# A recurrent attention layer with streamed weights: left K cast by ScalarE, left queries copied amid the Exp, results stored straight from SBUF, streamed units at new places

## The chip, the cores and the metric

The kernel runs on one core of a Trainium2 chip. Its time is the device time of one execution in microseconds (us), the median of several runs. The core has five instruction queues: TensorE (PE, with its weight loads as PEld), VectorE (DVE), ScalarE (ACT), GpSimd (POOL) and SyncE (SP), and sixteen DMA engines that all of them share. SBUF is the memory next to the engines, PSUM the one into which TensorE writes[...].

## The reference, cut to what matters

Two layers run on the same normed input and are added to it. The first is a recurrence over 64 segments of 32 rows; each segment puts 8 memory rows in front, and the first 8 rows of its result are the memory of the next. It has 32 heads of 128. The second is a dense layer with GELU.

```python
for s in range(n_seg):                        # 64 segments of 32 rows
    xs = x[:, s * seg_len:(s + 1) * seg_len, :].copy()
    h = jnp.concatenate([mem, xs], axis=1)    # 8 + 32 rows
    q = jnp.einsum('btd,dhe->bhte', h, Wq)
    k = jnp.einsum('btd,dhe->bhte', h, Wk)
    v = jnp.einsum('btd,dhe->bhte', h, Wv)
    scores = jnp.einsum('bhqe,bhke->bhqk', q, k) * scale
    scores = jnp.where(mask[None, None], scores, -1000000000.0)
    p = _softmax(scores, axis=-1)
    o = jnp.einsum('bhqk,bhke->bhqe', p, v)
    o = jnp.einsum('bhte,hed->btd', o, Wo)
    mem = o[:, :M, :].copy()                  # memory of the next segment
    outs.append(o[:, M:, :])
...
xn = _layernorm(x, axis=-1)
return x + _A_ref(xn, ...) + _B_ref(xn, ...)
```

## The kernel before

The four weight matrices of the recurrence (8 MB each in bf16) don't fit in SBUF. They are cut into 64 units of 128 x 2048 bf16, 512 KB each: eight units for each half of K, Q and V and sixteen for O. In each segment TensorE goes through all 64. 46 units stay in SBUF; 18 are streamed through six slots, in the order in which they are used. Two of the 18 are kept in PSUM banks and copied back by VectorE (`start_stream`, `kept_in`) rather than read from HBM, and one (`PART`) has 768 of its 2048 columns kept in SBUF, so that 320 KB of it are read. A slot takes its next unit once TensorE is done with the last (`unit_done`).

A segment's 32 rows are computed as 24 rows and 8 "left" rows. The 24 and the 8 memory rows go through in every segment. The left rows of four segments (a group; `i4` counts 0 to 3 in it) go together, one weight half at a time, each in one of the four segments: Q0 in i4 = 1, Q1 in i4 = 2, K0 and V1 in i4 = 3, K1 and V0 in i4 = 0, O in i4 = 1. So the four kinds of segment have different work. "Left K" is the K of those rows, "left queries" their Q.

```python
LEAD = 6
LATER = 3
STREAM_BUFS = 6
AT_BANKS, AT_PART = 5, 4
PART_COLS = 768
...
PLACED = "SS.....S" "....S..." ".S...S.." ".S.....S" "....S..." ".S.S..S." "...S.S.S" "..S..SS."
IS_STREAMED = {unit: PLACED[n] == "S" for n, unit in enumerate(ORDER)}
...
IN_PSUM = [unit for unit in ORDER if IS_STREAMED[unit]][3]
STREAMED_O = [unit for unit in ORDER[48:] if IS_STREAMED[unit]]

IN_BANKS, PART = STREAMED_O[AT_BANKS], STREAMED_O[AT_PART]
KEPT = (IN_PSUM, IN_BANKS)
...
            unit = UNIT_AT[place]
            res_tiles[unit] = slab(place)[:, :]
            fetch(res_tiles[unit], unit)


    streams = [unit for _ in range(NSEG) for unit in ORDER if IS_STREAMED[unit]]
...
    used = 0

    def copy_bits(out, in_):

        nc.vector.tensor_single_scalar(out=out, in_=in_, scalar=0, op=ALU.bitwise_or)

    def start_stream(slot):
        if not starts:
            return
        n = starts.popleft()
        unit, t = streams[n], slab(slot)
        if unit in kept_in:
            for c0, bank in kept_in[unit]:
                copy_bits(t[:, c0:c0 + 1024].bitcast(U32), bank.bitcast(U32))
        elif unit == PART:
            nc.sync.dma_start(out=t[:, PART_COLS:], in_=copies[unit])
        elif unit in copies:
            nc.sync.dma_start(out=t[:, :], in_=copies[unit])
        else:
            fetch(t[:, :], unit)
        stream_tiles[n], slot_of[n] = t, slot
```

The three accumulator banks go round: a pass takes one (two with left rows), and whoever reads it out lets it go. `turn` reads a bank out and transposes the result; `q_left` copies eight left queries per head beside the segment's own, `keep_q` copies the rest of them into spare columns of the PSUM bank `mixed`.

```python
            def turn(ps, home, cp):

                rows_out(ps, home, cp)
                nc.vector.transpose(out=home, in_=home)

            ...
            def turn_kL(ps, u):
                kL[u] = sp.tile([P, 16, 32], BF16, name=f"kL{u}")
                turn(ps, kL[u][:, :, :], nc.vector.tensor_copy)

            ...
            def q_left(u):

                if i4 >= 2 + u and more:
                    q = qS[:, i4 - 2 - u, :, :]
                else:
                    q = qL[u][:, :, NL * i4:NL * i4 + NL]
                nc.vector.tensor_copy(out=q_home[:, :, 0:NL], in_=q)

            ...
            def keep_q(u):

                n = 2 - u
                copy_bits(
                    mixed[:, 340:340 + 64 * n].bitcast(U32).rearrange("p (i h t) -> p h i t", i=n, h=16),
                    qL[u].bitcast(U32)[:, :, (GRP - n) * NL // 2:].rearrange("p h (i t) -> p h i t", i=n),
                )
```

Scores, the Exp and the masks (the Exp writes `pr_all`, a part of the buffer `half_home`); then the sums, whose result is written to `pd_main`. Scores and sums both use the PSUM bank `mixed`.

```python
            def scores(u):

                ... # 32 matmuls into mixed[:, 0:224], of kT, kL[u] and q_home
                pr = pr_all[:, 0:224]
                nc.scalar.activation(out=pr, in_=mixed[:, 0:224], func=ACT.Exp, scale=INV_SQRT_DH)
                prA = pr[:, 0:160].rearrange("p (c q) -> p c q", q=40)
                prB = pr[:, 160:224].rearrange("p (c q) -> p c q", q=16)
                for p, m in ((prA[:, :, NL:SEG], mask_order), (prB, mask_left[:, i4, :])):
                    n = m.shape[-1]
                    nc.vector.tensor_tensor(out=p, in0=p, in1=m[:, None, :].to_broadcast([P, 4, n]), op=ALU.min)
                st["pr", u] = prA, prB

...
            def sums(u):
                prA, prB = st["pr", u]
                ... # 8 matmuls into mixed[:, 0:160], of prA and prB
                nc.scalar.activation(out=mixed[:, 0:160], in_=mixed[:, 0:160], func=ACT.Ln)

                for b in (1, 0):
                    nc.scalar.activation(
                        out=mixed[:, 160 * b:160 * b + 160], in_=mixed[:, 0:160], func=ACT.Exp, scale=-1.0,
                        bias=off[:, b:b + 1],
                    )
                pdA = pd_main.rearrange("p (c b q) -> p c b q", c=4, b=2)
                ...
                nc.vector.tensor_tensor(
                    out=pdA.rearrange("p c b q -> p b c q"), in0=prA[:, None, :, :].to_broadcast([P, 2, 4, 40]),
                    in1=dd, op=ALU.mult,
                )
```

The order of a segment's passes. `at` names what is done after which unit of a pass.

```python
            turn_k(psK, 0)
            if first:
                turn_kL(psKL, 0)
            at = {} if first else {1: [lambda: q_left(0)]}
            if left_q[0] and not first:
                at[2] = [lambda: keep_q(0)]
            psQ, psQL = half_pass("Q", 0, left_q[0], at)
            if first:
                turn_qL(psQL, 0)
                q_left(0)
            turn_q(psQ)
            if left_q[0] and not first:
                turn_qL(psQL, 0)
            psK1, psK1L = half_pass("K", 1, left_k[1], {})
            st["kT", 1] = nat_home
            rows_out(psK1, nat_home, nc.scalar.copy)
            at = {
                0: [lambda: scores(0), lambda: nc.vector.transpose(out=nat_home, in_=nat_home)],
                6: [lambda: sums(0)],
            }
            if not first:
                at[1] = [lambda: q_left(1)]
                if left_q[1]:
                    at[2] = [lambda: keep_q(1)]
            if left_k[1]:
                at.setdefault(1, []).append(lambda: turn_kL(psK1L, 1))
            psQ1, psQ1L = half_pass("Q", 1, left_q[1], at)
            if first:
                turn_qL(psQ1L, 1)
                q_left(1)
            turn_q(psQ1)
            if left_k[0] and not first:
                turn_kL(psKL, 0)
            if left_q[1] and not first:
                turn_qL(psQ1L, 1)
            psV, psVL = half_pass("V", 0, left_v[0], {})
            st["V", 0] = values_out(psV, sp.tile([P, 512], BF16, name="v", tag="a"), nc.scalar.copy)
            if left_v[0]:
                left_values(0, psVL)
...
```

The end of a segment: the O pass, the memory rows of the next segment, and the results. In i4 = 1 the result of the left rows (`resL`, in `pr_all`) and that of the main rows go to a staging tensor in HBM and from there to the output; in i4 = 2 the main rows are staged too.

```python
            if i4 == 3:
                at.setdefault(2, []).append(rows_of_main)
...
                if n == 1 and left_o:
                    st["resL"] = pr_all
                    nc.gpsimd.dma_start(out=st["resL"][:, :], in_=hrL_d[og, :, 256:512])
            nw = 2 if left_o else 1
...
            res, rows = st["res"], slice(s * SEG, s * SEG + NX)
            tiles = (res, st["resL"]) if left_o else (res,)
            for w, r in reversed(list(enumerate(tiles))):
                nc.vector.tensor_tensor(out=r[:, :], in0=psX[:, 256 * w:256 * w + 256], in1=r[:, :], op=ALU.add)
                if left_o and not final:

                    for b in range(2):
                        c0 = 256 * (2 * b + w)
                        nc.gpsimd.dma_start(out=outL_d[og, :, c0:c0 + 256], in_=r[64 * b:64 * b + 64, :])
            let_go(psX)
...
            elif left_o:
                pairs = [(out_flat[rows, :], outL_d[og, m0:m0 + NX, :])]
                pairs += [
                    (out_flat[row:row + NL, :], outL_d[og, NL * sl:NL * sl + NL, :]) for sl, row in left_rows
                ]
                for o, r in pairs:
                    small.append(lambda o=o, r=r: nc.gpsimd.dma_start(out=o, in_=r))
            elif i4 == 2:
                nc.gpsimd.dma_start(out=outM_d[g, :, :], in_=res[:, :])
                o = out_flat[rows, :].rearrange("t (j c) -> j t c", j=4)
                r = outM_d[g, :, :].rearrange("(j t) c -> j t c", j=4)[:, 0:NX, :]
                rows_of_main = lambda o=o, r=r: nc.sync.dma_start(out=o, in_=r)
            else:
                for j in range(4):
                    nc.gpsimd.dma_start(out=out_flat[rows, 256 * j:256 * j + 256], in_=res[32 * j:32 * j + NX, :])
```

## Time and profile before

Three runs took 1886.43, 1886.92 and 1889.38 us. The profiled execution has a span of 1889.4 us.

| engine | busy us | share of the span | instructions |
|---|---|---|---|
| PE (matmul) | 1720.6 | 91% | 32208 |
| PEld (weight load) | 935.8 | 50% | 32228 |
| DVE | 917.8 | 49% | 2222 |
| ACT | 634.8 | 34% | 1352 |
| POOL | 234.2 | 12% | 464 |

The DMA engines moved 614.17 MB, 325 GB/s over the span. How to read the lines below: in the slices, each digit is the busy share of a fortieth of the span in tenths. A group of instructions is given by line of the kernel, engine, operation, and out<-in by the program's names. A wait is given as who waited for whom, and then the total in us, how often, and the longest. "L706" is the matmul of the projections (in `product`), L901 that of the O pass, L808 and L814 the scores, L833 and L839 the sums, L750 the cast in `rows_out`, L764 the transpose in `turn`, L786 the copy in `q_left`, L820 the Exp of the scores, L854 the write of `pd_main`, L241 VectorE's copy `copy_bits` (into `u`: a kept unit into its slot; into `mixed`: `keep_q`), L1005 the cast of the memory rows at a segment's end, which serves as the mark between segments.

### The profile page before, as it was taken

To read this page: it belongs to the slowest core of one execution; us is meant where nothing else is said; L and a number is where in the kernel's file an instruction comes from. 1 tells how busy PE (TensorE), PEld (TensorE's weight loads), DVE (VectorE), ACT (ScalarE), POOL (GpSimd) and SP (SyncE) were. 2 spreads that over 40 slices of the span, in tenths; PEclk is the share of its full clock that TensorE was granted. 3 is DMA by queue.
4 is the path that set the end of the run, shared out by engine and by line. 5 is a ranking of instruction groups with operands and counts; after the bars stand their busy time and mean duration, and the time that the engine had idled before them with its cause. 6 is when DMAs were issued, how large, how long until landed. Compare 5 with 4: busy or idle time off the path is not lost. (4 is left out here: it accounts for less than half of the span.)

```text
span 1889.4 us, 72759 instructions
## 1 busy us (share of the span) xinstructions
PE 1720.6 (91%) x32208; PEld 935.8 (50%) x32228; DVE 917.8 (49%) x2222; ACT 634.8 (34%) x1352; POOL 234.2 (12%) x464
## 2 busy tenths in 40 slices
PE   7999999998899898888989999999898888999987
PEld 3444444444454555545555555555555454545544
DVE  6657474614354444444444444444445454444443
ACT  6334352502233333333333333333233333333333
POOL 0000000001341111111111110111111111111111
PEclk9999999999999999999999999999999999999999
DMA  9821211599999999999999999999999999999998
GB/s 340 264 52 44 55 47 50 172 360 357 340 389 395 362 381 373 377 368 369 381 378 386 381 388 385 398 386 382 362 380 374 373 365 380 370 383 383 374 374 322
DMA packets 219672, 614.17 MB, mean 325 GB/s; under 512 B 45547, under 2 KB 65435, under 8 KB 219356
## 3 DMA queue, kind: packets, MB, share of 16 engines
q1 hardware_dynamic: 200892, 590.16, 82.9%
q0 software_dynamic: 14368, 16.71, 2.7%
q8 instruction: 252, 4.13, 0.9%
q10 hardware_dynamic: 4096, 2.64, 0.5%
q14 instruction: 64, 0.52, 0.1%
HBM read 595.19 MB, written 30.28 MB: 331 GB/s over the span
## 5 line engine op out<-in xcount | busy, mean ns | idle before, releaser
L706 PE MATMUL acc<-u,hr_home 128*32 128x512 bf16 x11520 | 782.6, 383 | 40.8 <-DMA u<-Wc_K 17.9
L706 PEld LDWEIGHTS <-hr_home 128*32 128x32 bf16 x12288 | 349.5, 97 | 324.1 <-issue 69.1
L706 PE MATMUL acc<-u,hrL 128*32 128x512 bf16 x2880 | 255.5, 380 | 31.2 <-DVE kL L750 19.5
L507 PE MATMUL ps<-u 128*128 128x512 bf16 x896 | 194.9, 380 | 2.6 <-ACT u L391 2.6
L901 PE MATMUL acc<-u,d_oL 128*32 128x256 bf16 (+1 forms) x3552 | 176.0, 290 | 12.2 <-DMA u<-Wc_O 7.1
L241 DVE TENSOR_SCALAR u<-kept 128x512 uint32<-128x512 uint32 x254 | 163.5, 685 | 37.5 <-PE acc L706 15.3
L901 PEld LDWEIGHTS <-b_oL 128*32 128x32 bf16 x3569 | 113.4, 99 | 70.0 <-issue 37.9
L556 PE MATMUL ps<-u 128*128 128x512 bf16 x657 | 146.2, 379 | 0.8
L854 DVE TENSOR_TENSOR pd_main<-half_home,mixed 128x320 bf16<-128x320 bf16 x128 | 61.9, 483 | 168.2 <-ACT mixed L847 166.5
L507 PEld LDWEIGHTS <-u 128*128 128x128 bf16 x896 | 87.8, 98 | 108.4 <-issue 3.4
L901 PEld LDWEIGHTS <-d_oL 128*32 128x32 bf16 (+1 forms) x3552 | 103.8, 98 | 62.7 <-issue 21.9
L706 PEld LDWEIGHTS <-hrL 128*32 128x32 bf16 x3072 | 89.2, 96 | 88.6 <-issue 52.1
L901 PE MATMUL acc<-u,b_oL 128*32 128x256 bf16 (+1 forms) x1618 | 107.7, 292 | 17.2 <-DMA u<-Wc_O 11.1
L764 DVE STREAM_TRANSPOSE b_oL<-b_oL 128x512 bf16<-128x512 bf16 x128 | 90.5, 707 | 64.6 <-ACT b_oL L750 64.6
L901 PE MATMUL acc<-W_O,b_oL 128*32 128x256 bf16 (+1 forms) x1776 | 109.2, 292 | 6.5 <-issue 6.2
L750 ACT CAST kT<-acc 128x512 bf16<-128x512 f32 x64 | 37.5, 586 | 228.9 <-PE acc L706 228.9
L263 POOL DMA_DIRECT2D hr_home<-hr_d x58 | 32.3, 557 | 636.4 <-PE acc L706 636.4
L750 ACT CAST b_oL<-acc 128x512 bf16<-128x512 f32 x128 | 75.2, 588 | 88.6 <-PE acc L706 87.7
L556 PEld LDWEIGHTS <-u 128*128 128x128 bf16 x672 | 65.3, 98 | 77.4 <-DVE g_u L523 0.4
L1005 ACT CAST d_oL<-acc 128x256 bf16<-128x256 f32 (+1 forms) x63 | 26.9, 427 | 213.7 <-PE acc L901 213.7
L847 ACT ACTIVATE mixed<-mixed,small_consts 128x160 f32<-128x160 f32 x256 | 94.2, 368 | 8.4
L515 ACT ACTIVATE g_xb<-ps,b1col 128x512 bf16<-128x512 f32 x112 | 76.8, 686 | 59.9 <-PE ps L507 58.8
(124 smaller groups left out, 1933.5 us busy)
## 6 DMA issues: line engine op xcount, KB each, us to landing
u<-Wc_K SPq DMA_DIRECT2D x320, 512.0 KB
u<-Wc_V SPq DMA_DIRECT2D x256, 512.0 KB
u<-Wc_O SPq DMA_DIRECT2D x256, 512.0 KB
u<-Wc_Q SPq DMA_DIRECT2D x128, 512.0 KB
u<-Wc_O SPq DMA_DIRECT2D x64, 320.0 KB
hr_home<-hr_d POOLq DMA_DIRECT2D x58, 128.0 KB, 5.5
u<-in_B_w_dram SPq DMA_DIRECT2D x14, 512.0 KB
u<-in_A_Wq_dram SPq DMA_DIRECT2D x14, 512.0 KB
```

The lines of the kernel that those rows point to most:

```text
L241: nc.vector.tensor_single_scalar(out=out, in_=in_, scalar=0, op=ALU.bitwise_or)
L263: eng.dma_start(out=hr_home[:, 0:n], in_=hr_d[s, :, 0:n])
L507: nc.tensor.matmul(ps[:, :].rearrange("p (s t) -> p s t", t=SEG), lhsT=w1_sb[fb // 14 * 8 + kt][:, (fb % 14) * P:(fb % 14 + 1) * P], rhs=x ...
L515: nc.scalar.activation(out=xb[:, :], in_=ps[:, :], func=ACT.Identity, bias=b1col[:, fb:fb + 1], scale=1.0)
L556: nc.tensor.matmul(ps[:, :], lhsT=gts[fc // 4][:, fc % 4, t * P:(t + 1) * P], rhs=w2_sb[fc // 2][:, fc % 2, cs], start=(fc == 0), stop=(fc ...
L706: nc.tensor.matmul(o, lhsT=lhs[:, i, :], rhs=m, start=(i == seq[0]), stop=(i == seq[-1]), tile_position=(0, 32 * j),)
L750: cp(out=out, in_=ps.rearrange("p (h e) -> p h e", e=32))
L764: nc.vector.transpose(out=home, in_=home)
L847: nc.scalar.activation(out=mixed[:, 160 * b:160 * b + 160], in_=mixed[:, 0:160], func=ACT.Exp, scale=-1.0, bias=off[:, b:b + 1],)
L854: nc.vector.tensor_tensor(out=pdA.rearrange("p c b q -> p b c q"), in0=prA[:, None, :, :].to_broadcast([P, 2, 4, 40]), in1=dd, op=ALU.mult,)
L901: nc.tensor.matmul(acc[r:r + n // 8, c:c + wide], lhsT=lhs[:, 4 * (i % 4) + 2 * u + k, :], rhs=w_t[:, c0 + c:c0 + c + wide], start=(unit = ...
L1005: nc.scalar.copy(out=o_sb[:, 0:no, :], in_=psX[:, 0:32 * no].rearrange("p (h e) -> p h e", e=32))
```

## The change

It has four parts.

- Left K is read out of PSUM by ScalarE instead of VectorE, and the K0 half is read out already after the second unit of the Q1 pass instead of after that pass, so that its bank is let go earlier.
- The left queries of the second half are copied by VectorE while ScalarE computes the Exp of the first half's scores, and the copy into `mixed` follows the masks directly; both stood one and two units later, behind the transpose of K.
- The two staging tensors in HBM are gone. Results are stored from SBUF to the output. The sum of the left rows is written to `pd_main`, and no longer in place, so that `pr_all` is free for the next Exp; four left row blocks, which lie 32 rows apart in the output, go in one DMA.
- The streamed units stand at other places in the segment, and the partly kept O unit is the fourth streamed one of the pass and no longer the fifth.

```diff
--- before.py
+++ after.py
@@ -51,7 +51,7 @@
 LEAD = 6
 LATER = 3
 STREAM_BUFS = 6
-AT_BANKS, AT_PART = 5, 4
+AT_BANKS, AT_PART = 5, 3
 PART_COLS = 768
 
 
@@ -70,7 +70,7 @@
 
 
 ORDER = pass_order()
-PLACED = "SS.....S" "....S..." ".S...S.." ".S.....S" "....S..." ".S.S..S." "...S.S.S" "..S..SS."
+PLACED = "SS.....S" "...S..S." "....S..." "...S...." "S..S...." "S.S...S." "..S..S.." "S.S..SS."
 IS_STREAMED = {unit: PLACED[n] == "S" for n, unit in enumerate(ORDER)}
 assert PLACED.count("S") == STREAMED
 RESIDENT = [unit for unit in ORDER if not IS_STREAMED[unit]]
@@ -122,8 +122,6 @@
     hr_d = dram.tile([NSEG + 1, P, 512], BF16, name="hr_d")
-    outL_d = dram.tile([NGRP, 2 * SEG, DM], BF16, name="outL_d")
-    outM_d = dram.tile([NGRP, P, 256], BF16, name="outM_d")
 ...
@@ -769,7 +767,7 @@
 
             def turn_kL(ps, u):
                 kL[u] = sp.tile([P, 16, 32], BF16, name=f"kL{u}")
-                turn(ps, kL[u][:, :, :], nc.vector.tensor_copy)
+                turn(ps, kL[u][:, :, :], nc.scalar.copy)
 
             def turn_q(ps):
                 turn(ps, q_home[:, :, NL:40], nc.scalar.copy)
@@ -797,7 +795,7 @@
                     qL[u].bitcast(U32)[:, :, (GRP - n) * NL // 2:].rearrange("p h (i t) -> p h i t", i=n),
                 )
 
-            def scores(u):
+            def scores(u, meanwhile=None):
 
                 kT, qL_ends = st["kT", u], ends(q_home)
                 sA = mixed[:, 0:160].rearrange("p (c q) -> p c q", q=40)
@@ -820,6 +818,8 @@
                 nc.scalar.activation(out=pr, in_=mixed[:, 0:224], func=ACT.Exp, scale=INV_SQRT_DH)
                 prA = pr[:, 0:160].rearrange("p (c q) -> p c q", q=40)
                 prB = pr[:, 160:224].rearrange("p (c q) -> p c q", q=16)
+                if meanwhile is not None:
+                    meanwhile()
                 for p, m in ((prA[:, :, NL:SEG], mask_order), (prB, mask_left[:, i4, :])):
                     n = m.shape[-1]
                     nc.vector.tensor_tensor(out=p, in0=p, in1=m[:, None, :].to_broadcast([P, 4, n]), op=ALU.min)
@@ -932,22 +932,20 @@
             st["kT", 1] = nat_home
             rows_out(psK1, nat_home, nc.scalar.copy)
             at = {
-                0: [lambda: scores(0), lambda: nc.vector.transpose(out=nat_home, in_=nat_home)],
+                0: [lambda: scores(0, None if first else lambda: q_left(1)), lambda: nc.vector.transpose(out=nat_home, in_=nat_home)],
                 6: [lambda: sums(0)],
             }
-            if not first:
-                at[1] = [lambda: q_left(1)]
-                if left_q[1]:
-                    at[2] = [lambda: keep_q(1)]
+            if left_q[1] and not first:
+                at[0].insert(1, lambda: keep_q(1))
             if left_k[1]:
-                at.setdefault(1, []).append(lambda: turn_kL(psK1L, 1))
+                at[1] = [lambda: turn_kL(psK1L, 1)]
+            elif left_k[0]:
+                at[1] = [lambda: turn_kL(psKL, 0)]
             psQ1, psQ1L = half_pass("Q", 1, left_q[1], at)
             if first:
                 turn_qL(psQ1L, 1)
                 q_left(1)
             turn_q(psQ1)
-            if left_k[0] and not first:
-                turn_kL(psKL, 0)
             if left_q[1] and not first:
                 turn_qL(psQ1L, 1)
             psV, psVL = half_pass("V", 0, left_v[0], {})
@@ -986,8 +984,6 @@
             if left_v[1] and not first:
                 at[9] = [lambda: left_values(1, psV1L)]
             at.setdefault(0, []).append(load_res)
-            if i4 == 3:
-                at.setdefault(2, []).append(rows_of_main)
             psX = new_acc()
             for n, unit in enumerate(O_UNITS):
                 t = unit_tile(unit)
@@ -1016,13 +1012,12 @@
                     lead_products(LEAD)
             res, rows = st["res"], slice(s * SEG, s * SEG + NX)
             tiles = (res, st["resL"]) if left_o else (res,)
-            for w, r in reversed(list(enumerate(tiles))):
-                nc.vector.tensor_tensor(out=r[:, :], in0=psX[:, 256 * w:256 * w + 256], in1=r[:, :], op=ALU.add)
-                if left_o and not final:
-
-                    for b in range(2):
-                        c0 = 256 * (2 * b + w)
-                        nc.gpsimd.dma_start(out=outL_d[og, :, c0:c0 + 256], in_=r[64 * b:64 * b + 64, :])
+            sums_at = (res, pd_main[:, 0:256])[:len(tiles)]
+            for w in reversed(range(len(tiles))):
+                nc.vector.tensor_tensor(
+                    out=sums_at[w][:, :], in0=psX[:, 256 * w:256 * w + 256], in1=tiles[w][:, :], op=ALU.add
+                )
+            tiles = sums_at
             let_go(psX)
             left_rows = [
                 (sl, (GRP * og - 2 + sl) * SEG + NX) for sl in range(GRP) if s - GRP < GRP * og - 2 + sl <= s
@@ -1042,17 +1037,20 @@
                             engines[n % 3].dma_start(out=out_flat[o, cs], in_=r[i, :])
                             n += 1
             elif left_o:
-                pairs = [(out_flat[rows, :], outL_d[og, m0:m0 + NX, :])]
-                pairs += [
-                    (out_flat[row:row + NL, :], outL_d[og, NL * sl:NL * sl + NL, :]) for sl, row in left_rows
-                ]
-                for o, r in pairs:
-                    small.append(lambda o=o, r=r: nc.gpsimd.dma_start(out=o, in_=r))
-            elif i4 == 2:
-                nc.gpsimd.dma_start(out=outM_d[g, :, :], in_=res[:, :])
-                o = out_flat[rows, :].rearrange("t (j c) -> j t c", j=4)
-                r = outM_d[g, :, :].rearrange("(j t) c -> j t c", j=4)[:, 0:NX, :]
-                rows_of_main = lambda o=o, r=r: nc.sync.dma_start(out=o, in_=r)
+                of_seg = out_flat.rearrange("(g t) d -> g t d", t=SEG)
+                for w, r in reversed(list(enumerate(tiles))):
+                    for b in range(2):
+                        c0 = 256 * (2 * b + w)
+                        cs = slice(c0, c0 + 256)
+                        p0 = 64 * b + m0
+                        nc.gpsimd.dma_start(out=out_flat[rows, cs], in_=r[p0:p0 + NX, :])
+                        if len(left_rows) == GRP:
+                            o = of_seg[GRP * og - 2:GRP * og - 2 + GRP, NX:SEG, cs]
+                            nc.gpsimd.dma_start(out=o, in_=r[64 * b:64 * b + SEG, :])
+                        else:
+                            for sl, row in left_rows:
+                                p0 = 64 * b + NL * sl
+                                nc.gpsimd.dma_start(out=out_flat[row:row + NL, cs], in_=r[p0:p0 + NL, :])
             else:
                 for j in range(4):
                     nc.gpsimd.dma_start(out=out_flat[rows, 256 * j:256 * j + 256], in_=res[32 * j:32 * j + NX, :])
```

## The prediction

> **What bounds the kernel now.** I read the page from the top. Its slices show two stages: a first quarter in which the dense layer fills TensorE and the DMA digits are low, and then the recurrence, from about 430 us to the end, in which both rows stand at 9.
>
> ```profile
> PE   7999999998899898888989999999898888999987
> DMA  9821211599999999999999999999999999999998
> q1 hardware_dynamic: 200892, 590.16, 82.9%
> ```
>
> The change touches only the recurrence, so I asked for the busy time of one group of four segments (segments 32 to 35, one line each, which are of the kinds i4 = 0, 1, 2, 3) and of 62 segments together (from the first cast of the memory rows, line 1005, to the last).
>
> ```profile
> core 0: us, PE busy (x) PEld busy (x) DVE busy (x) ACT busy (x) POOL busy (x), PEclk, DMA share, GB/s
> 1162.10:1184.30 22.20, 20.22 (x510) 12.16 (x506) 10.77 (x25) 7.26 (x17) 2.61 (x5) 1.00 1.01 391
> 1184.30:1206.00 21.70, 21.38 (x413) 11.69 (x409) 10.39 (x25) 7.26 (x17) 3.14 (x6) 1.00 1.03 405
> 1206.00:1225.90 19.90, 18.45 (x484) 10.56 (x486) 10.46 (x26) 7.58 (x17) 5.23 (x10) 1.00 1.02 396
> 1225.90:1249.70 23.80, 21.24 (x511) 12.11 (x507) 10.77 (x25) 7.29 (x18) 1.11 (x2) 1.00 1.01 387
> 455.30:1861.20 1405.90, 1268.20 (x29280) 722.68 (x29280) 653.90 (x1560) 455.14 (x1054) 218.33 (x412) 0.99 1.00 378
> ```
>
> The last line is the key one. A segment takes 1405.9 / 62 = 22.7 us. TensorE is idle 1405.9 - 1268.2 = 137.7 us of it, 2.2 us a segment, and the DMA share is 1.00. So two resources are nearly full at once. A share of 1.00 can hide small pauses[...]; counting the packet records of segments 6 to 62 myself, the sixteen DMA engines together stand idle 0.56 us of a mean segment of 22.55 us. The DMA is thus 2.5% from its own floor, TensorE some 10%. VectorE and ScalarE are at 47% and 32%: they matter only where TensorE waits for a single one of their instructions.
>
> What TensorE waits for in those 62 segments:
>
> ```profile
> PE acc L706 <- DVE kL L750: 19.5, 30, 1.0
> PE acc L901 <- DMA u<-Wc_O: 18.3, 39, 1.8
> PE acc L706 <- DMA u<-Wc_K: 17.3, 27, 2.0
> PE mixed L833 <- DVE mixed L241: 12.3, 15, 1.9
> PE mixed L808 <- DVE b_oL L764: 8.9, 29, 0.4
> PE mixed L833 <- DVE b_oL L786: 3.9, 13, 0.3
> ```
>
> Columns: total us, times, longest. The first is a projection that needs the PSUM bank from which VectorE has still to cast the left K. The fourth and sixth are the first matmul of the sums, which waits for VectorE to finish copying left queries. These three are what the change aims at: 19.5 + 12.3 + 3.9 = 35.7 us. The DMA lines, 36 us, say that the streamed weights already come late at times.
>
> One wait sits further back, in ScalarE, before the Exp of the scores:
>
> ```profile
>   DMA outL_d<-half_home: 8.2, 9
> ```
>
> In segments of the kind i4 = 2 the Exp must overwrite the place from which the left results are still being staged. In the trace the staging issues 1.95 us after the segment's start and lands at 6.7 to 8.3 us (first piece), and the Exp starts at 7.3 to 9.0 us. This delays the masks, the query copies behind them and so the fourth wait above.
>
> [...] with one stream queue at 82.9% the share is 1.00. So removing staging copies gives time to the weights. [...] the direct stores have rows of 256 bf16, which is just 512 B, and so had the staging writes (256-column slices of a 1024-column tensor); [...] the 1024 B packets of that queue take 46 ns. [...] The trace has 665 and 586 ns for these casts, so moving the cast gains 0.08 us itself; the queue it leaves matters more. [...] I therefore argue from waits and not from 91%.
>
> **Part 1, left K on ScalarE and early.** There are 32 casts of 0.665 us; they leave VectorE (21 us of its busy time). In i4 = 3 the cast stood after the whole Q pass, behind a query transpose (0.707 us); the waiting projection lost 1.0 us in segment 35. In i4 = 0 it stood behind the transpose of K and the query copy; 0.35 us lost in segments 32 and 36. After, both casts run on ScalarE at unit 1 of the Q pass, right after the Exp (0.36 us). The sums come at unit 6; a unit without left rows takes about 0.24 us (32 matmuls of eight units in 1.91 us at 1010 us), so ScalarE has 5 x 0.24 = 1.2 us, the cast takes 0.59 and ends before Ln. The bank is free some 1.5 us before the V pass. I take the whole 19.5 us.
>
> **Part 2, query copy amid the Exp.** The copy (0.15 to 0.19 us) runs while ScalarE does the Exp (0.36 us); it needs only the scores' reading done. The second copy (0.22 us) comes ahead of the transpose of K (0.70 us). In segment 34 VectorE ran masks 1214.22, transpose 1214.44, copy 1215.07, second copy 1215.14 to 1215.36, and the sums began at 1215.41, 0.68 us late. Without the transpose in between, and with the query copy gone forward, the sums are released about 0.85 us sooner. 12.3 + 3.9 = 16 us of waits go. The transpose itself is wanted only in the V pass.
>
> **Part 3, direct stores.** By the listed sizes one group moved 4 x 32 KB to the left staging, 48 + 4 x 16 KB out of it, 64 KB to the other staging and 48 KB out: 352 KB. Now it is 4 x 12 + 4 x 16 KB and 4 x 12 KB, 160 KB. The 192 KB saved at 378 GB/s are 0.52 us a group, 8 us for fifteen to sixteen groups. The 8.2 us of ScalarE's wait vanish with it, but lie behind part 2's wait and are not counted again. The new wait is that the next probabilities overwrite `pd_main` while four stores still read it. Four issues of 0.55 us starting at 1.95 us landed by 8.5 to 9.8 us; line 854 now starts at 9.7 to 12.1 us, and would come up to 1.5 us sooner. So 0 to 0.3 us in sixteen segments, 2 us lost.
>
> **Part 4, places of the streamed units.** Still eighteen per segment, six of them in the O pass, two kept in PSUM and one shorter by 192 KB, so the bytes do not change. Over the passes K0, Q0, K1, Q1, V0, V1, O the counts go from 3, 1, 2, 2, 1, 3, 6 to 3, 2, 1, 1, 2, 3, 6. One thing can be worked out: the copy of the last kept unit (O unit 14) may start once the unit three streams earlier is done. That was O unit 7 and becomes unit 8. Before, the two copies (2 x 0.685 us) ended 0.72 us before the segment's end in i4 = 0 and 3, and unit 14 began at -0.65 us: no slack. One unit of 0.24 us less costs about 0.15 us in two kinds of segment: 32 x 0.15 = 5 us lost. In i4 = 3 VectorE was itself busy up to then, so it should not change.
>
> **The sum.** If TensorE alone set the pace: -35.7 - 2 (Exp, other casts) + 2 + 5 = -31 us. If the DMA alone did: -8 us, for the DMA moves 16 streams whatever TensorE does. In truth the DMA pauses only 0.56 us a segment, 35 us in all, because TensorE's stalls keep slots occupied. Of TensorE's 137.7 us idle some 40 are waits for weights themselves, so stalls of its own are about 98 us, and 36 of those go: 37%. If the DMA's pauses shrink in that proportion, that is 13 us; with the 8 us of bytes saved, 21; less a few for the late copy, 19. Predicted 1886.9 - 19 = 1868 us.
>
> **Rivals.** (a) The DMA is the bound and each stall removed turns into a wait for weights: 1879 us. For it: share 1.00, and 36 us of DMA waits. Against: segment 36 took 20.1 us at a share of 0.99, so the packets can run faster than the mean. (b) The stalls convert in full and the places were well chosen: TensorE's -31 us and some of the 36 us of weight waits, 1850 us. For it: the waits are clear and repeat each group. Against: the 2.5% of DMA pauses would have to go nearly whole. (c) New waits eat the gain: late stores into `pd_main`, the copy of the kept unit, eight stores in one burst ahead of the next rows on GpSimd's queue (8 x 0.53 us, then 5.3 us landing, about 12 us into a segment, while the next rows are loaded at about 17 us): 1885 us or more.
>
> **Range and chances.** (a) and (b) lie 11 and 18 us to each side; the range 1853 to 1881 holds most of both. Faster by over 2% needs below 1849.2 us, which is beyond the sum for TensorE: 0.07. Slower by over 2% needs 38 us of new waits, for which nothing speaks: 0.02.
>
> **What would show it.** In the profile after, the three waits of part 1 and 2 should be gone or under 5 us together, ScalarE some 19 us busier and VectorE 21 less, DMA bytes lower by about 3 x 1 MB (16 x 192 KB), and TensorE's waits for `Wc_` tiles should have grown from 36 us: by about 12 us if I am right, by 30 if (a) is. A wait of TensorE for VectorE's copy into `u` ahead of the last O units near 5 us is part 4's cost. I am wrong if `pd_main` waits for stores, or if the weight waits shrink, which would mean that the new places, and not the stalls, decide.

## The result, and the profile after

The changed kernel takes 1933.06 us (median of four runs, 1930.14 to 1933.87), the kernel before 1888.15 us (1886.43 to 1891.38) in the same comparison: a ratio of 1.0233, with a 95% interval of 1.0214 to 1.0252. The prediction was 1868 us, in a range of 1853 to 1881. The change cost 45 us where it was to bring 19. Repeated beside one of the later runs it gave 1.019 (1.0152 to 1.0229).

The slices and the stream queue of the page after:

```profile
PE   7999999998898978888988989898989898999887
q1 hardware_dynamic: 199292, 589.38, 81.7%
DMA packets 219290, 611.06 MB, mean 316 GB/s; under 512 B 47388, under 2 KB 66348, under 8 KB 218973
```

The row of TensorE has 17 eights and a seven from the eleventh slice on, where it had 13 eights before, and the bytes went down from 614.17 to 611.06 MB, as part 3 meant them to. So there is less to move, and yet it takes longer. The same group as before (segments 32 to 35), a line each, and the 62 segments together. The columns are those of the windows in the prediction; the granted clock stands third from the end:

```profile
1186.20:1208.90 22.70, 20.45 (x511) 12.29 (x507) 10.34 (x24) 7.80 (x19) 2.58 (x5) 1.00 1.01 391
1208.90:1231.00 22.10, 21.14 (x413) 11.08 (x409) 10.29 (x25) 7.25 (x17) 3.12 (x6) 1.00 1.02 392
1231.00:1255.10 24.10, 20.55 (x487) 11.75 (x491) 10.75 (x26) 7.54 (x18) 5.13 (x9) 0.86 0.94 326
1255.10:1279.00 23.90, 21.30 (x512) 12.11 (x508) 10.27 (x24) 7.78 (x19) 2.58 (x5) 1.00 0.99 383
455.40:1901.40 1446.00, 1282.89 (x29280) 724.69 (x29280) 642.22 (x1530) 469.96 (x1084) 240.67 (x447) 0.97 0.97 365
```

The third line is the segment of the kind i4 = 2. It took 19.90 us before and takes 24.10 now; its DMA share is down to 0.94 and its clock to 0.86. This group shows more than the rule: on average over the last 54 segments those of i4 = 2 went from 21.3 to 23.3 us and those of i4 = 3 from 22.9 to 24.1, and the other two kinds were no longer than before. Over all, 1446.0 us stand against 1405.9. Of these 40.1 us, 25.4 are idle time of TensorE (1446.0 - 1282.9 = 163.1, before 137.7), and 14.7 are the same 29280 matmuls taking longer (1282.9 against 1268.2). Both columns will need a cause.

What TensorE waits for in the recurrence after:

```profile
PE mixed L806 <- DVE b_oL L762: 56.0, 30, 4.4
PE acc L704 <- DVE hr_home L288: 18.6, 9, 6.4
PE acc L901 <- DVE u L239: 9.4, 31, 0.5
PE acc L704 <- DMA u<-Wc_K: 9.2, 20, 1.3
PE acc L704 <- DMA u<-Wc_V: 3.9, 11, 0.7
PE acc L901 <- DMA u<-Wc_O: 3.8, 8, 1.1
```

(L806 is the scores' matmul, L808 before; L762 the transpose of the queries, L288 the cast of the next rows' transposed x, L239 the copy `copy_bits`. TensorE's lines with "issue", idle time for which the trace names no cause, and one single wait of 5.4 us are left out.) The three waits that the change aimed at (19.5, 12.3 and 3.9 us) are gone from the list. In their place stands one of 56.0 us, up to 4.4 us at a time, which was 8.9 us before: the scores wait for VectorE's transpose of the second half's queries. The waits for weights have shrunk. The second line, 18.6 us where it was 3.6, is the wait for the next segment's rows. Why VectorE is late is seen in its own list and in GpSimd's:

```profile
POOL out_dram L1049 <- issue: 65.5, 28, 5.4
DVE pd_main L854 <- DMA out_dram<-pd_main: 58.5, 13, 6.1
POOL out_dram L1046 <- issue: 56.9, 18, 4.3
DVE hr_home L288 <- DMA hr_home<-hr_d: 33.1, 10, 7.9
```

The second line is the wait that part 3 of the prediction put at 2 us: VectorE can't write the probabilities into `pd_main` until the stores that read it are done. It is 58.5 us, 13 times; two more of the same kind, 9.0 us, stand under "issue", so that all fifteen segments of i4 = 2 from segment 6 on have it. The first and third lines tell why: GpSimd, which issues those stores, stands still for 122 us before them with "issue", that is, with nothing that the profile shows as its cause. GpSimd's timeline in segment 34, whose mark is at 1231.0 us:

```profile
1233.07 0.52 POOL L1046 DMA_DIRECT2D out_dram<-pd_main  x1 [7.02 <-DVE hr_home L1017]
1233.74 0.63 POOL L1049 DMA_DIRECT2D out_dram<-pd_main  x1
1234.36 0.53 POOL L1046 DMA_DIRECT2D out_dram<-pd_main  x1
1238.40 0.62 POOL L1049 DMA_DIRECT2D out_dram<-pd_main  x1 [3.51 <-issue]
1239.02 0.51 POOL L1046 DMA_DIRECT2D out_dram<-hr_home  x1
1240.12 0.62 POOL L1049 DMA_DIRECT2D out_dram<-hr_home  x1 [0.59 <-issue]
1244.29 0.52 POOL L1046 DMA_DIRECT2D out_dram<-hr_home  x1 [3.54 <-issue]
1245.06 0.61 POOL L1049 DMA_DIRECT2D out_dram<-hr_home  x1 [0.25 <-issue]
```

L1046 are stores of main rows, L1049 those of four left row blocks. Three go out in a row, then there is a pause of 3.51 us ahead of the fourth, the last that reads `pd_main`, and a second pause of 3.54 us ahead of the seventh. The first store had landed at 1238.10; the fourth is issued 0.30 us later. VectorE in the same stretch:

```profile
1239.23 0.70 DVE L935 STREAM_TRANSPOSE d_oL<-d_oL 128x512 bf16<-128x512 bf16 x1
1244.10 0.49 DVE L854 TENSOR_TENSOR pd_main<-half_home,mixed 128x320 bf16<-128x320 bf16 x1 [4.17 <-DMA out_dram<-pd_main]
1244.71 0.71 DVE L762 STREAM_TRANSPOSE b_oL<-b_oL 128x512 bf16<-128x512 bf16 x1
```

It idles 4.17 us until the fourth store has landed, at 1243.98, and the transpose for which TensorE waits comes behind it. The late stores delay the next rows too: their load overwrites `hr_home`, out of which the last stores read, and in these segments it goes out 0.6 to 1.4 us after the last of them has landed, at 18.3 to 22.5 us of the segment (14.7 to 16.4 before).

### The profile page after: what moved, and what is told of

Read it like the earlier page. It is cut to its first block, busy times and chain, and to the rows that moved or that the text cites. A ratio compares the mean times of both kernels' runs of the same rounds, so it can differ in the third digit from the quotient of the medians.

```text
span 1930.7 us, 72886 instructions
## 1 busy us (share of the span) xinstructions
PE 1738.9 (90%) x32228; PEld 937.7 (49%) x32228; DVE 905.1 (47%) x2190; ACT 650.6 (34%) x1384; POOL 257.9 (13%) x502
## 2 busy tenths in 40 slices
DMA packets 219290, 611.06 MB, mean 316 GB/s; under 512 B 47388, under 2 KB 66348, under 8 KB 218973
## 3 DMA queue, kind: packets, MB, share of 16 engines
q10 hardware_dynamic: 4096, 2.64, 0.4%
## 5 line engine op out<-in xcount | busy, mean ns | idle before, releaser
L704 PE MATMUL acc<-u,hr_home 128*32 128x512 bf16 x11520 | 806.2, 389 | 55.1 <-DVE hr_home L288 18.6
L704 PEld LDWEIGHTS <-hr_home 128*32 128x32 bf16 x12288 | 350.0, 98 | 358.4 <-issue 76.3
L704 PE MATMUL acc<-u,hrL 128*32 128x512 bf16 x2880 | 260.2, 382 | 11.2 <-issue 6.6
L239 DVE TENSOR_SCALAR u<-kept 128x512 uint32<-128x512 uint32 x254 | 163.6, 686 | 47.6 <-PE acc L901 28.0
L901 PE MATMUL acc<-u,d_oL 128*32 128x256 bf16 (+1 forms) x3552 | 176.5, 298 | 9.5 <-issue 9.5
L901 PEld LDWEIGHTS <-b_oL 128*32 128x32 bf16 x3569 | 111.0, 98 | 68.6 <-issue 34.1
L901 PEld LDWEIGHTS <-d_oL 128*32 128x32 bf16 (+1 forms) x3552 | 106.5, 102 | 61.0 <-issue 16.1
L1056 POOL DMA_DIRECT2D out_dram<-hr_home x188 | 95.3, 509 | 298.6 <-DVE hr_home L1017 287.4
L901 PE MATMUL acc<-u,b_oL 128*32 128x256 bf16 (+1 forms) x1618 | 110.6, 290 | 16.3 <-DVE u L239 9.4
L762 DVE STREAM_TRANSPOSE b_oL<-b_oL 128x512 bf16<-128x512 bf16 x128 | 90.6, 708 | 72.9 <-ACT b_oL L748 72.9
L704 PEld LDWEIGHTS <-hrL 128*32 128x32 bf16 x3072 | 88.5, 96 | 61.1 <-issue 22.4
L901 PE MATMUL acc<-W_O,b_oL 128*32 128x256 bf16 (+1 forms) x1776 | 107.6, 289 | 4.7 <-issue 4.5
L752 ACT CAST v<-acc 128x512 bf16<-128x512 f32 x128 | 75.1, 587 | 65.4 <-PE acc L704 64.2
```

What stands on the lines that cost most here:

```text
L704: nc.tensor.matmul(o, lhsT=lhs[:, i, :], rhs=m, start=(i == seq[0]), stop=(i == seq[-1]), tile_position=(0, 32 * j),)
L752: cp(out=t[:, :], in_=ps[:, :])
L901: nc.tensor.matmul(acc[r:r + n // 8, c:c + wide], lhsT=lhs[:, 4 * (i % 4) + 2 * u + k, :], rhs=w_t[:, c0 + c:c0 + c + wide], start=(unit = ...
```

## The experiments

The theory formed from this: GpSimd's DMA queue is full. The program sets aside `SCRATCH = 384` bytes per partition for that queue (`nc.dynamic_dma_scratch_size = SCRATCH`), and eight stores ahead of each other don't fit. The pause comes from that, VectorE's wait from the pause, and TensorE's from VectorE's. Rivals: the new places of the units are what costs (part 4), the stores themselves are slow or disturb the weights, or it is the granted clock.

### Room for the queue, another issuing engine, the old places, the old staging

Four kernels on one chip, where the kernel before took 1896.53 us. The first gives the queue more room. SBUF is full, so something has to go: one resident O unit keeps 1536 of its 2048 columns, and its last 512 columns are taken from its own columns 1024 to 1535 a second time. `pd_main` moves into the space so gained. Matmuls and streamed bytes stay the same in number, but a quarter of that unit's product is left out.

```diff
-SCRATCH = 384
-SMALL = 3712
+SCRATCH = 1024
+SMALL = 3072
```

> The changed kernel, with the buffer for GpSimd's DMA descriptors at 1024 bytes per partition instead of 384; pd_main lies elsewhere in SBUF, and to make room one resident O unit has only 1536 of its 2048 columns loaded, the last 512 being taken twice from the same unit (same matmuls, another result). Theory A: all eight stores of a segment i4 = 1 go out back to back (issue gaps about 0.55 to 0.66 us, none above 1 us), the last of pd_main lands by 9.5 us, the wait at line 854 is under 8 us, and the time is 1870 us (1858 to 1885), the same as with ScalarE issuing. Theory B: 1915 to 1935 us. Theory C (late landing in itself): issues go out at once but the wait at 854 stays above 30 us.

The second lets ScalarE issue the stores of the left row blocks.

```diff
-                            nc.gpsimd.dma_start(out=o, in_=r[64 * b:64 * b + SEG, :])
+                            nc.scalar.dma_start(out=o, in_=r[64 * b:64 * b + SEG, :])
```

> The changed kernel, with the stores of four left blocks (4x8x256) issued by ScalarE instead of GpSimd; same bytes, same places. Theory A (room in GpSimd's DMA queue: in the changed kernel GpSimd issues three stores at 1.95, 2.6 and 3.2 us of a segment and the fourth only 0.30 us after the first has landed, at about 7.4; the last store of pd_main then lands at 12.5 to 14.8 us and line 854 waits for it): GpSimd keeps only the main-row stores and issues them without a pause, VectorE's wait at line 854 for stores of pd_main falls from 58.5 us to under 8, segments of kind i4 = 2 fall from 23.4 us to about 21, and the time is 1870 us (1858 to 1885). Theory B (the new places of the streamed units cost the time): stays at 1915 to 1935 us, though the wait at 854 may go. Theory C (stores from SBUF land late whoever issues them, because the DMA engines are full): the wait at 854 stays above 30 us and the time above 1905 us.

The third puts the streamed units back to their old places (`PLACED` and `AT_PART` of before), the fourth brings the two staging tensors back and keeps parts 1, 2 and 4.

> The changed kernel with the streamed units and the partly kept unit at the places of before; parts 1 to 3 stay. Theory A: the wait at 854 stays near 55 us and the time within 1915 to 1945 us, for the places decide little. Theory B (the places are the cause): 1870 to 1890 us.

> The changed kernel with the results staged through HBM as before (left sum in place, both staging tensors), that is parts 1, 2 and 4 alone. Theory A: no wait for stores of pd_main, GpSimd's issues as in the kernel before, TensorE's waits of before for left K (19.5 us) and the query copies (12.3 and 3.9 us) gone for the most part: 1875 us (1862 to 1890). Theory B: 1915 us or more.

| kernel | us | ratio to before (95%) |
|---|---|---|
| more room | 1868.40 | 0.9848 (0.9829 to 0.9868) |
| left stores from ScalarE | 1884.98 | 0.9929 (0.9907 to 0.9951) |
| old places | 1921.58 | 1.0140 (1.0101 to 1.0178) |
| staged as before | 1886.82 | 0.9945 (0.9925 to 0.9965) |

More room turns the loss of 2.3% into a gain of 1.5%. With the old places 1.4% of loss remain, so part 4 isn't the main cause. With the staging, which means without part 3, the loss is gone. GpSimd's timeline of the kernel with more room in its segment 34 (mark at 1189.0):

```profile
1190.84 0.52 POOL L1054 DMA_DIRECT2D out_dram<-pd_main  x1 [6.74 <-DVE pd_main L1025]
1191.40 0.64 POOL L1057 DMA_DIRECT2D out_dram<-pd_main  x1
1192.04 0.53 POOL L1054 DMA_DIRECT2D out_dram<-pd_main  x1
1192.57 0.62 POOL L1057 DMA_DIRECT2D out_dram<-pd_main  x1
...
1195.10 0.61 POOL L1057 DMA_DIRECT2D out_dram<-hr_home  x1 [0.22 <-issue]
```

All eight go out one behind the other within 4.9 us. The last of `pd_main` lands at 8.4 to 10.5 us of a segment, and the profile shows no wait of VectorE's write of `pd_main` (L861 there) for a store. In one segment of fifteen, 38, the write starts 0.13 us after the landing, with 1.67 us of idle time before it in place of the usual 1.12, so that there some 0.5 us may be such a wait. Its 62 segments together, and TensorE's waits (L813, L769, L909 and L711 are L806, L762, L901 and L704 of the kernel after):

```profile
454.80:1838.40 1383.60, 1268.26 (x29280) 726.06 (x29280) 642.49 (x1530) 470.15 (x1085) 239.36 (x447) 1.00 1.00 382
```

```profile
PE acc L909 <- DMA u<-Wc_O: 17.4, 38, 1.0
PE acc L909 <- DVE u L239: 7.2, 24, 0.5
PE mixed L813 <- DVE b_oL L769: 7.0, 26, 0.4
PE acc L711 <- DMA u<-Wc_V: 5.3, 12, 0.9
PE acc L711 <- DMA u<-Wc_K: 5.0, 10, 1.5
```

The 56.0 us have become 7.0. The matmuls are back at 1268.3 us in sum, which is what they took before, and TensorE's idle time is at 1383.6 - 1268.3 = 115.3 us. So the 62.4 us between these two kernels are 47.8 of idle time and 14.6 of slower matmuls; both go with the pause.

The kernel with ScalarE's stores, which computes everything, gets 0.7% and not 1.5%. In its segment 34 ScalarE spends four issues of 0.63 us from 1.57 to 4.43 us on them, so that its cast of K begins 4.52 us into the segment (3.77 with more room). And its first eight segments take 185.2 us, with more room 177.7 (189.0 before, 190.2 after). These account for 7.5 of the 16.6 us between the two; that the rest is ScalarE's is argued, and a run further down speaks against it.

### Each part alone, and the room alone

Four kernels on another chip (before: 1891.03 us): before with parts 1 and 2; before with part 4; before with more room; parts 1 to 3 with more room and the old places. The edits are hunks of the change's diff and of the one above; the two with more room leave out the same quarter of a unit.

> The kernel before with parts 1 and 2 alone (left K on ScalarE and early, query copies amid the Exp); staging and places as before. If the stalls of TensorE that these parts take away (35.7 us) convert as I summed them, the ratio to before is 0.992 to 0.996 (7 to 15 us less). If every stall only turns into a wait for weights: 0.998 to 1.002. The same with the new places gave 0.9945; the difference to this run is part 4.

> The kernel before with part 4 alone, the new places of the streamed units. My reading: the places decide little once no stall of several us stands in the segment, so 0.997 to 1.004. If the places by themselves cost what old_places seemed to show (1.014 there against 1.0233 for the changed kernel): 1.007 to 1.011. If they were chosen well: below 0.995.

> The kernel before with the descriptor buffer of GpSimd's DMA queue at 1024 bytes per partition instead of 384 (pd_main elsewhere, one resident O unit with its last 512 columns taken twice). Theory A says that the queue's room also holds up the first segments of the kernel before, where the results of the dense layer are spread by small copies (GpSimd idle 40.2 us before those copies with no wait that the profile shows, segment 2 takes 27.8 us): these pauses go, segment 2 takes about 22 us, and the ratio is 0.994 to 0.997. If the gain of ring64 came only from the stores: 0.999 to 1.001.

> Parts 1 to 3 with the large descriptor buffer and the old places of the streamed units. With ring64 at 0.9848: if the places decide little, 0.983 to 0.988; if the new ones cost time, below 0.982; if they gain, above 0.989.

| kernel | us | ratio to before (95%) |
|---|---|---|
| before + parts 1, 2 | 1880.41 | 0.9939 (0.9917 to 0.9961) |
| before + part 4 | 1898.29 | 1.0044 (1.0026 to 1.0061) |
| before + more room | 1885.93 | 0.9975 (0.9957 to 0.9993) |
| parts 1 to 3 + more room | 1874.13 | 0.9909 (0.9872 to 0.9945) |

Parts 1 and 2 bring 0.61%, 11.5 us. Part 4 alone costs 0.44%. Before gains a little from more room too: its first eight segments take 179.9 us with it and 189.0 without, in the later 54 they hardly differ (1214.1 and 1216.9). What went are these pauses of GpSimd in the kernel before, ahead of the small copies of the dense layer's result:

```profile
POOL hr_d L455 <- issue: 32.3, 12, 4.4
POOL hrL_d L455 <- issue: 7.9, 7, 3.9
```

With more room 0.2 us of them are left (the ratio, 0.9975, lies between the two ranges expected). So the queue was already at its limit there, in a place that the prediction didn't look at. The whole change with more room against before with more room is 0.9848 / 0.9975 = 0.987, about -24 us, give or take 5 (the two were measured on different chips, each beside the kernel before). Without part 4 it is 0.9909 / 0.9975 = 0.993, -12 us, on one chip.

Part 4 isn't the same in every company. With parts 1 to 3 and room it seems to bring something (0.9848 against 0.9909, the intervals just apart, on different chips), with parts 1 and 2 alone nothing (0.9945 against 0.9939), alone it costs, and with parts 1 to 3 without room it costs too (1.0233, or 1.0190 when repeated, against 1.0140). How the places play together with the other parts stays open.

### How the queue counts

A way of counting that fits the runs so far, an estimate: a store takes as many places of the room as it has rows on the DMA engine that carries most of them, and one more. By the packet records a store of 24 main rows goes as 12 packets of 1024 B, two rows each, and the one of four left blocks as four packets of 4096 B, eight rows each. The records don't name the engine; with one packet an engine the first goes over 12 engines and takes 3, the second over only four and takes 9. Three stores are 3 + 9 + 3 = 15, and a fourth of 9 would make 24: it was held. Once the first had landed it went, with 21 then in flight. The fifth then waits for the second, the sixth for the third, and so on; in segment 42 the landings at 6.78 and 7.64 us are followed by issues at 7.09 and 7.94. So by this count 384 bytes hold at least 21 places and fewer than 24. The one more for each store is not shown: without it these stores fit as well, with at least 18 places and fewer than 20.

Four kernels test it (before: 1891.35 us): one-block stores in place of those of four blocks; two-block ones; the kernel before with 256 bytes of room, where its four staging stores of 64 rows (counted as four rows on each of 16 engines, so 5 places each, 20 in all) shouldn't fit, two thirds of 21 to 23 places being 14 to 15; and the two left stores that read `pd_main` issued by ScalarE, the others by GpSimd.

```diff
-                        if len(left_rows) == GRP:
+                        if False:
```

> The changed kernel, with each store of four left blocks made as four stores of one block (8 rows of 512 B). The same bytes in more instructions. Theory A as a count: [...] a store takes as many as the busiest of its DMA engines has rows, plus one. A main store (24 rows on 12 engines, from its 1024 B packets) takes 3, a four-block store (8 rows on each of 4 engines, 4096 B packets) takes 9, a one-block store 2. So the ten stores of pd_main take 2 x (3 + 8) = 22 and go out without a pause from 1.95 us on, 0.53 us apart; the last lands near 12 us, so line 854 waits some 2 us instead of 4.5 and the total of that wait falls from 58.5 to about 30 us. Time 1900 us (1885 to 1915), between the changed kernel and left_act. If it is the number of stores in flight and not their shape that fills the queue, GpSimd still pauses after the third store, and it gets slower: above 1940 us.

```diff
-                            o = of_seg[GRP * og - 2:GRP * og - 2 + GRP, NX:SEG, cs]
-                            nc.gpsimd.dma_start(out=o, in_=r[64 * b:64 * b + SEG, :])
+                            for k in (0, 2):
+                                o = of_seg[GRP * og - 2 + k:GRP * og + k, NX:SEG, cs]
+                                p0 = 64 * b + NL * k
+                                nc.gpsimd.dma_start(out=o, in_=r[p0:p0 + 2 * NL, :])
```

> The changed kernel, with each store of four left blocks made as two stores of two blocks. By the count of theory A each takes as much room as one of four blocks (8 rows on each of 2 engines, 9 places), half the bytes: [...] the fourth store, a main one, already waits for the first to land, and the buffer is full for longer: the wait at 854 grows from 58.5 us to 90 us or more and the time to 1950 us or more. If bytes or stores filled the queue, it would be as in the changed kernel or better.

```diff
-SCRATCH = 384
-SMALL = 3712
+SCRATCH = 256
+SMALL = 3840
```

> The kernel before with the descriptor buffer at 256 bytes per partition instead of 384. [...] the four staging stores (64 rows on 16 engines) take 5 each, 20 in all. So in segments i4 = 2 the fourth staging store, which went out at 3.62 us of the segment, now goes out 0.30 us after the first has landed, near 7.2 us. [...] If the count is wrong: still 3.62 us.

```diff
-                            nc.gpsimd.dma_start(out=o, in_=r[64 * b:64 * b + SEG, :])
+                            (nc.scalar if w else nc.gpsimd).dma_start(out=o, in_=r[64 * b:64 * b + SEG, :])
```

> The changed kernel, with only the two left stores of pd_main issued by ScalarE and the other six stores of the segment by GpSimd. In left_act ScalarE was busy with four issues from 1.57 to 4.42 us, and the cast of K began at 4.5 us; with two it is free at 2.9 us. By the count GpSimd's stores take 3 + 3 + 3 + 9 + 3 = 21 places, so only its last waits, which nothing needs soon. Expected 0.988 to 0.992 of before (left_act had 0.9929, the large buffer 0.9848).

| kernel | us | ratio to before (95%) |
|---|---|---|
| one-block stores | 1938.88 | 1.0250 (1.0211 to 1.0289) |
| two-block stores | 2019.21 | a single run |
| before, room of 256 B | 1994.28 | a single run |
| ScalarE issues two left stores | 1880.35 | 0.9949 (0.9930 to 0.9967) |

The kernel before with 256 bytes now has the disease of the kernel after. GpSimd's timeline, segment 34 (mark at 1268.4):

```profile
1273.75 1.11 POOL L1025 DMA_DIRECT2D outL_d<-half_home  x2 [5.71 <-DVE half_home L1020]
1274.85 0.53 POOL L1025 DMA_DIRECT2D outL_d<-hr_home  x1
1277.40 0.54 POOL L1025 DMA_DIRECT2D outL_d<-hr_home  x1 [2.01 <-issue]
```

Three staging stores go out, and the fourth 0.31 us after the first has landed at 1277.09. In three more such segments the pairs of landing and issue are 9.49 and 9.81, 8.59 and 8.90, 8.69 and 9.00 us. Two-block stores have, counted in the same way, eight rows on each of two engines, so they take 9 as well, and there are more of them: the fourth store is again issued 0.31 us after the first landing. With two left stores on ScalarE, the count lets five go (3 + 3 + 3 + 9 + 3 = 21) and holds the sixth, of 9, until three have landed: it was issued at 7.89, 8.79, 8.71 and 8.34 us, the third landings being at 7.54, 8.44, 8.36 and 7.99. There the pause delays no store of `pd_main`, and the kernel is 0.5% faster than before. But 0.988 to 0.992 was expected, since ScalarE has only half of the issues that it had with all left stores (0.9929). So ScalarE's issues aren't shown to be what that kernel loses against the one with more room.

One-block stores take 2 each by the count, and the ten stores of `pd_main` 22, so that all ten were expected to go out at once. It was eight:

```profile
1229.45 0.52 POOL L1046 DMA_DIRECT2D out_dram<-pd_main  x1 [7.18 <-DVE hr_home L1017]
1229.96 2.03 POOL L1053 DMA_DIRECT2D out_dram<-pd_main  x4
1231.98 0.52 POOL L1046 DMA_DIRECT2D out_dram<-pd_main  x1
1232.48 1.00 POOL L1053 DMA_DIRECT2D out_dram<-pd_main  x2
1234.29 0.51 POOL L1053 DMA_DIRECT2D out_dram<-pd_main  x1 [0.81 <-DMA out_dram<-pd_main]
```

The ninth waits for a DMA, and here the profile names it. That is a second limit, and one of the program: it has eight semaphores for GpSimd's DMAs (in the trace of the kernel after 458 DMAs use eight in turn, 57 or 58 each), and each store waits for that of the one eight before it. Twenty short stores run into it twice, VectorE's write of `pd_main` starts at 12.6 to 14.9 us of a segment, and nothing is won. The expectation failed by this second limit. That a one-block store takes 2 places is thus not shown.

### Other ways round, and the clock

With nearly every pause TensorE's granted clock falls to 0.50: in 12 of the 15 segments in the same segment, in two more in the next. The windows of the kernel after in segment 34: up to the end of VectorE's wait, behind it, and the rest.

```profile
1231.00:1243.90 12.90, 11.22 (x252) 5.73 (x253) 5.04 (x13) 4.72 (x10) 3.43 (x6) 1.00 0.98 366
1243.90:1251.00 7.10, 5.54 (x116) 3.09 (x119) 3.93 (x10) 2.39 (x6) 1.70 (x3) 0.53 0.85 295
1251.00:1255.10 4.10, 3.80 (x127) 2.93 (x123) 1.78 (x3) 0.43 (x2) 0.00 (x0) 0.98 0.95 253
```

The second line has 116 matmuls in 5.54 us of busy time at a clock of 0.53, 48 ns each, where the third has 30 (the kinds of matmul are mixed in both). The trace's clock records show stretches of 3.4 or 6.8 us at 0.50 (but for the last one, which the end of the run cuts off): 6 of them, 26.9 us together, before; 20, 87.7 us, after; 5, 19.3 us, with more room. The stretches go with idle time: of 20 stops of TensorE of 2 us or more in the recurrence, 17 have one begin 1.4 to 4.8 us after their start. Seven of these 17 stops were shorter than the 3.4 us of a stretch, 2.0 to 3.36 us. In segment 34 TensorE stood still from 1242.2 to 1245.5, and the clock fell at 1244.3.

Is the loss that of the pause, or of the clock behind it? The next kernels fill the pause with 48 matmuls of 512 columns, whose product nobody reads, ahead of the scores of the second half in i4 = 2. The first writes them into the next accumulator bank, the second into the one after it. Measured beside the first: the left stores from SyncE, as another way round.

```diff
+                if u == 1 and i4 == 2:
+                    spare = new_acc()          # second kernel: after free_banks.rotate(1)
+                    for k in range(48):
+                        ... # a matmul of 512 columns into spare
+                    let_go(spare)
```

> The changed kernel, and in each segment i4 = 2, ahead of the second scores, 48 matmuls more into a PSUM bank that nobody reads, on a resident unit: about 3 us of work at the place where TensorE stands still for 3.7 us. Nothing else is moved; the wait for the stores of pd_main stays (58.5 us at line 854). Open question: of the 40.1 us more between the first and last segment mark, 25.4 us are idle time of TensorE and 14.7 us are the same matmuls taking longer, at a granted clock of 0.97 instead of 0.99. If the half-clock stretches of 3.4 or 6.8 us that follow the pause in nearly every segment i4 = 2 are the pause's consequence, filling it removes them: the mean clock goes back to 0.985 or more, and the time falls by 8 to 20 us, to a ratio of 1.012 to 1.019 of before. If they have another cause: clock near 0.978 and ratio 1.022 to 1.030.

> The changed kernel with the four stores of left blocks issued by SyncE, whose queue otherwise issues the weights. In left_act the four issues (0.63 us each) kept ScalarE from the cast of K until 4.5 us of the segment and it got 0.9929; the large buffer, with the same stores, 0.9848. If ScalarE's delay is the difference, SyncE gives 0.984 to 0.989. If it is that weights behind the stores start later, or if GpSimd's room in the first segments makes the difference (small copies of the dense result, 7.5 us more in segments 1 to 8): 0.990 to 0.996.

> As fill, with the 48 extra matmuls going into a bank that ScalarE has let go already, so that they run in the pause and not behind it (in fill they waited for a bank that VectorE frees after line 854, and so came on top of the pause). If the half-clock stretches are the consequence of the pause: they go from most segments i4 = 2, the mean clock is 0.985 or more, and the ratio to before is 1.012 to 1.019, against 1.0233 for the changed kernel. If they have another cause: clock near 0.978, ratio 1.022 to 1.030.

> The changed kernel itself, beside fill2 on the same chip: 1.019 to 1.027, mean clock 0.975 to 0.982.

| kernel | us | before there | ratio (95%) |
|---|---|---|---|
| pause filled, next bank | 1982.02 | 1891.36 | 1.0466 (1.0416 to 1.0516) |
| left stores from SyncE | 1894.51 | 1891.36 | 1.0019 (0.9998 to 1.0039) |
| pause filled, bank after | 1949.47 | 1894.71 | 1.0300 (1.0230 to 1.0371) |
| the change again | 1930.39 | 1894.71 | 1.0190 (1.0152 to 1.0229) |

The first filling failed as a test: its bank was still to be read by a cast that stands behind VectorE's write of `pd_main`, so that the added matmuls waited for the pause themselves and ran behind it, and slower (median 631 ns each in place of 379). The second ran inside it. Its windows: segment 34 up to VectorE's write of `pd_main` and behind it, then the start of segment 35 (mark 1262.4) in two pieces.

```profile
1241.00:1253.10 12.10, 11.71 (x264) 6.02 (x260) 5.11 (x14) 4.71 (x10) 3.44 (x6) 1.00 1.02 399
1253.10:1260.00 6.90, 6.90 (x212) 4.51 (x208) 4.46 (x11) 2.75 (x7) 1.14 (x2) 1.00 0.89 325
1262.40:1266.10 3.70, 1.09 (x28) 0.28 (x20) 0.00 (x0) 0.37 (x1) 0.00 (x0) 0.99 0.99 371
1266.10:1272.90 6.80, 5.78 (x56) 2.25 (x60) 2.53 (x5) 0.59 (x1) 2.02 (x4) 0.50 0.70 253
```

The half clock has left segment 34 and stands in segment 35, behind a new stop of TensorE there. None of the fifteen segments of i4 = 2 from segment 6 on has such a stretch any more, and eight of those behind them have one early on. So it goes where the stop goes. But the time didn't fall: the ratio is 1.0300, where 1.012 to 1.019 was expected if the stretches follow the pause. VectorE still waits 52.0 us for the stores, the last stores still land late (at 18.3 us in segment 34), the next rows are loaded only behind them (from 19.3 us), and TensorE meets that at the start of the next segment:

```profile
PE acc L704 <- DVE hr_home L288: 38.7, 17, 3.9
```

The segments of i4 = 2 take 22.2 us there (23.3 after), those of i4 = 3 26.3 (24.1). Hiding the stop of TensorE doesn't take the delay away. In the windows 14.7 of the 40.1 us are slower matmuls; what the pause alone would cost isn't separated by these runs, as none had the same stops of TensorE at full clock.

With the left stores on SyncE, GpSimd's pause is gone as well, but SyncE issues the stream of weights, and that stands behind the stores:

```profile
SPq L1049 <- DVE hr_home L1017: 28.5, 15, 3.6
```

SyncE waits 28.5 us for the sums, and TensorE waits 22.2 us for V units and 22.3 us for O units that come late (2.8 and 16.9 with ScalarE issuing). The gain of the other parts is spent: neither of the ranges expected held.

## Why the prediction was wrong, point by point

**Part 3, "0 to 0.3 us in sixteen segments, 2 us lost": this step failed.** It measured 58.5 us of waiting on VectorE. Some 49 us of it reached TensorE (56.0 us in that line, against 7.0 with more room), with the next rows' 18.6 us (3.6 before) and some 15 us of slower matmuls behind them. The prediction had named this as its sign of being wrong, "if `pd_main` waits for stores". The step took the four staging issues of before, 0.55 us each from 1.95 us on, as a pattern for the new stores and let them land by 8.5 to 9.8 us. With more room that is what happens: the four of `pd_main` land by 8.4 to 10.5 us, and next to nobody waits. What the step left out is that the queue holds only so many stores. The four staging stores fit (5 places each, 20 by the count, where 21 did fit). Of the new ones every second takes 9 by the same count, its 4 x 8 rows going as only four packets. That it is the room is shown, by the runs with 1024 and 256 bytes; the count itself only fits. The rival (c) named "eight stores in one burst" and looked at the time that the issues take (8 x 0.53 us), not at what they need to be in flight together (it also put the load of the next rows at about 17 us; in the kernel before it went out at 14.7 to 16.4 us in these segments); "slower by over 2%" was given a chance of 0.02 because nothing was seen that spoke for it.

**Part 3, bytes and the Exp's wait: right; the 8 us for the bytes: not shown.** 3.1 MB fewer were moved, and the Exp no longer waits for a staging store. But on one chip parts 1 to 3 with more room stand at 0.993 of before with more room, and parts 1 and 2 alone at 0.994 of before. That leaves about 1 us for part 3 with enough room, with some 9 us of uncertainty, so that 8 isn't excluded either.

**Part 1: right.** The wait of 19.5 us is gone; 32 casts of 21.3 us in sum left VectorE and came to ScalarE as 18.8 us. The busy times moved by less: over the 62 segments VectorE's fell by 11.7 us and ScalarE's rose by 14.8, where 21 and 19 were expected.

**Part 2: right.** The waits of 12.3 and 3.9 us are gone. Both parts together brought 11.5 us (7 to 16 by the interval), where the prediction turned 36 us of waits into 13 us of time. The number held, the step to it is not borne out: counted from the packet records as in the prediction, the pauses of the DMA fell from 0.56 to 0.43 us a segment in the kernel with parts 1 and 2 (one trace each), by 22% or some 8 us and not by 37% or 13.

**Part 4: the place of its wait right, its size about half, the effect unsettled.** TensorE's wait for the copy into `u` is 9.4 us, 31 times (0.9 us before), where 5 us in 32 segments were expected. Alone the places cost 0.44%, 8 us; with parts 1 to 3 and room they seem to bring some 11 us.

**Waits for weights: wrong.** They were to grow from 36 us by about 12. They shrank: K, V and O give 9.2 + 3.9 + 3.8 = 16.9 us, and Q another 2.6; counted like that it was 40.0 us before. That goes with the pause, as TensorE comes later to them: with parts 1 to 3 and the old places the sum is 20.7 us with the pause and 35.5 us with more room. With parts 1 and 2 alone, which take the stalls away and add nothing, it is 34.0 us, so there too it didn't grow. TensorE's stops for which the trace names no cause ("issue") did: in the recurrence 40.0 us before, 58.5 us with parts 1 and 2, 64.2 us with the whole change and more room. What they wait for is not known, so it stays open how much of the stalls taken away went into late weights after all. With more room, where the time is the best, K, V and O give 5.0 + 5.3 + 17.4 = 27.7 us, and TensorE's idle time is lower by 22.4 us than before (115.3 against 137.7). The prediction's last sentence, that shrinking weight waits would mean that the new places decide, isn't borne out: the places alone bring these waits from 40.0 to 27.4 us, and the kernel is slower with it.

**The sum.** With the queue's room equal on both sides the change is worth some 24 us, and 19 were predicted. That these are near each other is in part luck: parts 1 and 2 came out as summed (11.5 us for 13), but the bytes brought about 1 us for 8, and the places seem to have brought some 11 us where a cost of 5 was put. One term, the new wait, was put at 2 us and made the outcome.

## What to carry to other kernels

Before many small stores are put in a row on one queue, count what each needs to be in flight, by its shape: a store of four blocks is one instruction, but by the count above took three times the room of a plain one. Look at whether a pause of the issuing engine begins at the same store each time and ends a fixed time (here 0.3 us) after an earlier one lands; the profile calls such a pause "issue" and names no cause. If the queue can't be given room, a few stores from another engine are the cheap way round, but the engine that takes them is held up: 0.63 us of ScalarE for each issue, or a late stream of weights on SyncE, which waited 28.5 us.

## What was not expected of the hardware

- With 384 bytes of room GpSimd stops issuing without a recorded wait (3.51 and 3.54 us in segment 34; 0.22 us with 1024 bytes) and goes on 0.30 to 0.35 us after an earlier DMA has landed. That the room counts by rows on the busiest DMA engine, with one place more per store, is an estimate that fits the runs (by it 15 places went out at once and 20 didn't with 256 bytes, 21 and 24 with 384), no more than that.
- The kernel before was at this limit too, in its first eight segments: 9.1 of its 189.0 us there went with more room.
- A stop of TensorE can cost a second time: 17 of the 20 stops of 2.0 to 6.4 us in the kernel after were followed by a granted clock of 0.50 for 3.4 or 6.8 us, and seven of those 17 stops were shorter than 3.4 us.
- Of kernels that compute everything, four beat both: left stores on ScalarE (0.9929), parts 1 and 2 alone (0.9939), parts 1, 2 and 4 (0.9945) and two left stores on ScalarE (0.9949), whose intervals overlap. The fastest that ran, with more room at 0.9848, leaves a part of one product out, and a version that finds those 640 bytes elsewhere was not run.
